# A new order of all steps, and new engines for the elementwise steps, in a kernel of attention and a softplus MLP

## The chip, the cores and the metric

The kernel runs on 1 core of one Trainium2 chip. The metric is device time in microseconds (us), the median of several runs. The profile is one execution, taken by the hardware profiler; its engines are PE (TensorE's matmuls), PEld (its weight loads), DVE (VectorE), ACT (ScalarE), POOL (GpSimd) and SP (SyncE, which issues the DMAs here).

## The reference

Two parts: attention in both directions between 512 tokens and 32 state rows per head, and a two-layer MLP with softplus over all 8 x 544 rows.

```python
def _attn_ref(x, state):               # B, H, S, Ns, D = 8, 8, 512, 32, 64
    scale = 1.0 / np.sqrt(D)
    scores = scale * np.matmul(x, state.transpose(0, 1, 3, 2))
    scores = scores - scores.max(-1, keepdims=True)
    a = np.exp(scores)
    a /= a.sum(-1, keepdims=True) + 1e-09
    xread = np.matmul(a, state)
    scores2 = scale * np.matmul(state, x.transpose(0, 1, 3, 2))
    scores2 = scores2 - scores2.max(-1, keepdims=True)
    a2 = np.exp(scores2)
    a2 /= a2.sum(-1, keepdims=True) + 1e-09
    sread = np.matmul(a2, x)
    return np.concatenate([xread, sread], axis=2).astype(np.float32)

def _moe_ref(x, w_in, w_out):          # x: (8 * 544 rows, 512), d_ff = 2048
    h = x @ w_in
    g = np.maximum(h, 0.0) + np.log1p(np.exp(-np.abs(h)))
    return (g @ w_out).astype(np.float32)

def reference(**kwargs):
...
    x = np.ascontiguousarray(attn_out.transpose(0, 2, 1, 3)).reshape(B * S, H * D)
    return _moe_ref(x=x, **moe_kwargs)
```

The weights w_in and w_out are float64 in memory.

## The kernel before

The work is cut into steps, each of them one or a few instructions on one engine. A step has a letter; each letter stands for a generator function that makes its steps one after another (first g, second g, and so on). The string PLAN names all 1565 steps of the kernel by their letters, in one order. The last loop of the function goes through PLAN and lets the named generator make its next step. Every instruction goes through a helper (line 84) that keeps it in this order on its engine; so each engine, and the DMA queue of SyncE, works off its own steps strictly in the order of PLAN, and waits between engines come only from data and from buffers. No wait holds two engines apart that share no data.

For the letters that stand in ENG, the table gives the engine of each single step: A is ScalarE, D is VectorE, P is GpSimd. All other letters have a fixed engine.

The steps, by what they do:

- Loads (SyncE): S state, T the transposed tokens xT, X the tokens, I w_in, O w_out, in pieces of mostly 512 KB. The weights are loaded as float64 words.
- Weights: the float64 words are made into float32 in three steps. For w_in: a (ScalarE, upper word), b (VectorE, lower word), c (VectorE, joins both into W). For w_out: A, B, C in the same way. Then D makes the rounded high part of w_out (float32r) and E the rest of it, low part, as D by the engine of ENG.
- Scores of one batch: Q (TensorE). Towards tokens: 1 (transpose of 32 x 32 blocks on VectorE), 2 (maximum), 3 (subtract), 4 (exponential), 5 (sum and reciprocal), 6 (multiply), 7 (transpose back), 8 and 9 (high and low part). Towards state: e (maximum), f (exponential), i (reciprocal), t (transpose on TensorE), u (copy), R (matmul with the tokens), r (scale), y (transpose on TensorE), z and Z (high and low part).
- The first product is not computed as (a @ state) @ w_in; v multiplies the state with W (TensorE), h and l split the result into high and low part, and g (gemm1) multiplies that with the attention weights. A product of two split operands takes three matmuls (high x high, high x low, low x high), so one g of 512 columns is six matmuls.
- s is softplus (ScalarE) from PSUM to SBUF, m and n its high and low part, G (gemm2) the second product, two G for one g, each six matmuls; o copies a finished bank of PSUM to SBUF and p stores it.
- For the state rows, w and x split w_in itself, and eight g of 24 matmuls multiply it with the state read.

The order of slots (one slot is a g, an s, an m, an n and two G) is fixed in SLOTS: 16 slots of 128 hidden columns each for batch 0, then batch 1 and so on; before the last batch, the eight slots of the state rows. So batch 0 needs all of w_in and w_out within its 16 slots.

Buffers are rooms with names, taken in the order in which they came free: 27 of 2 KB per partition (tiles s in the profile), 26 of 4 KB (tiles d: raw loads, a's split parts, the split w_out), 5 small ones (v), and 8 banks of PSUM (b). W is the joined w_in, ST the state. With another order, a step can get another room, and so wait for another step.

```python
    run = {k: f() for k, f in steps.items()}
    for k in PLAN:
        now[0] = k
        count[k] = count.get(k, 0) + 1
        next(run[k])
```

Of the kernel before, what the change touches and what calls it, by code (L numbers as in the profile page):

```python
# [19 lines left out]
B, H, S, NS, D = 8, 8, 512, 32, 64  # L20
# [12 lines left out]
UNITS = {0: [(0, 256), (256, 512), (512, 1024), (1024, 1536), (1536, 2048)]}  # L33
UNIT = [(512 * c, 512 * c + 512) for c in range(4)]
PLAN = (
    "STTIQa112eIX2bb345e34ftf6t5a7ccI6uv897XOIIau8ihRiblOa9hlaIcbBgAIgscIvOBCsRhmhlDrlgbAcIrbaCDObcEnbamgIAOGGcacsI"
    "BOnvbsIyOTIChAEhDlIlbEBGmCAnIGOBgmagcCaGaaBbcsgssOAmDIncGBbcgaCaEvnAhDbGmACDazEGBlZCDhlbGsGgnaEmXcOAgAbBgOScGB"
    "AbssmcCnDTsmOEcQBEB1DXT2envO3hfeflnCAEGGGOG1OgihlDtsGECGB4mOuADgAAstT56GCmm2CgnD7sBuv3ERhRn4lir89G5g6EhCAmGn7G"
    "lG8gnmSDrysvzmhnTlEBDGshmElGQGTB1CZ9geg1GDssCEneGm2G34fmgDggsGnnfs5tuEGsnGopGvoohv67ilmmogng2smntmunh3gslmGXG4"
    "igGGhGlnsGhmgG8s5GGXnlTsnRmRrvhGlmgs6grhGGGlgsn7ynmvn9p8smzngZmGGgssGGGhgGlhG9mlsmpGgmGngsnsgmmnGnsgQs1ev2GeGG"  # L40
    "GGhGlmnpf3nGG1holgmpGgssotmgs4nnGfm2GGm34gGsgGoGG5nGToumv5shvnnXmhGGlhpGi6TgGnGsmGng7l6lsGgmng8nisSs9hgtmGGuGn"
    "GGGpmXXG7G8glssmmngGvRnsR9hGlgsGghGlrnsmGrgsvGgXmhpmlggnGGsoThGysoolvQsnhl1e2gGzspZggnef3om4snG1hf5GGggGisGstm"
    "6mmg2ls3nu4GGmtusmmgnGingpGGRRmnsrrm7nvGGGhmGg5nGmh6snp7mpsXGvlhn8yzmG9GGhGGZn8Gl9lngsGmnvhGgnllgGsghGssmggGlX"
    "Q1emTssfvnGTGnheGgomoGnolgs2ogs341GGnGsp5fGgmGg2st6mnmgmnhmGlnsTGsGmnt3pgpuguGn7isGg4smsmmnGgigs56RrRrv7snhmX8"
    "h8vmXGlGGGGG9plnGG9nGGnGgsmhGmgsngsmhnGlmnvyGlGhlzGhGGnggGXZsgGolmGspmvholsoQTn1geegh1sfgslnGn2Gm3ns42GGmGtupg"
    "gomnfgs3tGGGinG4msGgnGGssmimGmn5GnGuGvR5hpRw6lnGG7mgGrGs6GGvm8h9rlnyg7shGgnzGsGxmn8m9GglnhsgmsGGGGnlpgGmsZGooQ"
    "o1vpvhlmmgsp2eowgfnef1gphgssntnglhmGlGpG3nmGmsxmG2hsiG4G3igtGnnw5lunXmx4GwGngsgsggmuGGn6sssGxggG7Gs5RRrm8rwv9y"
    "GxGsGnzmgZGhwsgnwhlmGnGGm6xmGsnnmng7mgxwwsGGxsnwGmxwwG8GgGxmGmxwGnwsnolGxonmGpgxwsgxoxomGGsgGmnnw9sxggGvmvsshh"
    "vGGGlGGnmpnGglsgnmsGgpGhsmgGsnGGmonGmlmhGlGgGnsnhglGgGmGGsomnGgshlGsggmnsGnmnGsgpmgGGnnGgsGGmmGnGssGGgnGGmnGgG"
    "smsnmmGpGnGGnGGoGoooppppp"  # L50
)
ENG = {
    '3': "PPPDDPDPPPDDPDDD",
    '6': "PPPDPPDDPPPDDDDD",
    '8': "APADAPDAAPDADADA",
    '9': "PDDPDPPPPDPPPDPD",
    'D': "PDPPDPPPDPPDAPDA",
    'E': "PPDPPDPPPDPDPDDP",
    'h': "AAAAADAADDAAADDADDDDADAADDDDADDDAAAAAADDDDDADAAAADDADDAAADDDDAAAAD",
    'm': "DPPPDPPPDADPADPDPDPPPPADPAPADPPPDAAPPAPDDADDADAPDDPAADDPPPPAAPADPDPPPDAPDADADADDAPPPAAPPPDPAPPDDPAPAPAPPDPPPPADPADADAAAPDAADAAAAAPDDPDDP",  # L60
    'n': "PDPDPDPDPPPPPDPPDDPPDDDDPDDDDPPDDDPPPDPDPPDPPPPDDPPDPPDDDPDPPPPDPDDDDDDPPPDDPDPDPPPPPDPDDDPDPDDPPPDPPDDDDPPPPPDDPDPPPPDDPPPDDPPPDDDPDPDD",
    'o': "ADAADDAAAADADAADDDAAAAADDAAAADAAAA",
    'r': "DDDDAAAADDDDAAAD",
    'u': "AAAAAADADDADDDDA",
    'w': "DPPDPPDAAPDPPDPD",
    'x': "DDPDDDPDPPPDDPPD",
    'z': "AAAADAAA",
}


# [635 lines left out]
```

## Time and profile before

| | before |
|---|---|
| median of 3 runs | 671.09 us (670.12 to 671.17) |
| the profiled execution | 670.02 us, span 668.2 us |
| TensorE busy | 646.5 us (97%), 3856 matmuls |
| VectorE busy | 293.3 us (44%), 515 instructions |
| ScalarE busy | 249.8 us (37%), 398 instructions, 49 of them table loads |
| GpSimd busy | 204.2 us (31%), 197 instructions |
| read and written | 34.60 MB and 8.91 MB |
| granted TensorE clock | 1.0 |

The span goes from the first to the last instruction of the program. In a group's row stand the line, the engine, the operation, the tiles out<-in, the shape and the count; behind the bar the busy time in us and the mean ns of one; behind the second bar the idle time of the engine just before them, and whose end closed most of it. A row of a table by stretches has the stretch and its length, then for each engine the busy time and the count in the order PE, PEld, DVE, ACT, POOL, then the clock, the DMA engines' share and GB/s. All steps have line 84, that of the helper, so they are told apart by tiles and operations.

### The profile page before, as it was taken

How to read it: one execution, taken by the hardware profiler on the slowest of the kernel's cores; microseconds unless marked ns; L12 is line 12 of the kernel's file. 1: busy time of each engine (PE TensorE's matmuls, PEld its weight loads, DVE VectorE, ACT ScalarE, POOL GpSimd, SP SyncE). 2: the span in 40 equal slices, each digit the busy share in tenths (PEclk: the TensorE clock that was granted, in tenths of full speed). 3: DMA queues.
4: the chain of work that ended last, by engine and by line, in shares of the span. 5: the costliest groups of instructions: out<-in, count | busy, mean ns of one | idle time of the engine just before them, and what ended most of it. 6: DMA issues, size and time to landing. Idle time of an engine off the chain costs nothing.

```text
span 668.2 us, 9510 instructions
## 1 busy us (share of the span) xinstructions
PE 646.5 (97%) x3856; PEld 498.5 (75%) x3856; DVE 293.3 (44%) x515; ACT 249.8 (37%) x398; POOL 204.2 (31%) x197
## 2 busy tenths in 40 slices
PE   2999999999999999999999999999999999999997
PEld 0555767777787877777778777877778798888886
DVE  4999987444325312543264421434265153222110
ACT  2876755622332312732265321811263121313201
POOL 2545553312131420334211411411241456211210
PEclk9999999999999999999999999999999999999999
DMA  8995110500042020301030201100110000001001
GB/s 313 410 404 206 53 32 1 158 1 0 1 141 96 0 79 5 123 26 38 0 112 1 79 0 55 41 0 2 42 53 1 1 1 31 32 1 32 0 1 63
DMA packets 15851, 44.12 MB, mean 66 GB/s; under 512 B 1728, under 2 KB 2752, under 8 KB 15808
## 3 DMA queue, kind: packets, MB, share of 16 engines
q1 hardware_dynamic: 15808, 43.52, 18.3%
q8 instruction: 30, 0.49, 0.3%
q14 instruction: 13, 0.11, 0.0%
HBM read 34.60 MB, written 8.91 MB: 65 GB/s over the span
## 4 chain that ended last, share of the span: by engine, by line
PE 88%; DVE 9%; issue 1%; DMA 1%; ACT 1%; SPq 0%; DVEq 0%
PE b L84 88%; DVE s L84 6%; DVE W L84 1%; DVE v L84 1%; DVE d L84 1%; DMA d<-in_xt_dram 1%; ACT s L84 0%; ACT L84 0%; SPq L84 0%; DVE sreadT L84 0%; DVEq L84 0%
## 5 line engine op out<-in xcount | busy, mean ns | idle before, releaser
L84 PE MATMUL b<-d,s 128*128 128x512 f32 (+1 forms) x2912 | 568.5, 363 | 1.9 <-DVE v L84 1.6
L84 PEld LDWEIGHTS b<-d,s 128*128 128x128 f32 (+1 forms) x2912 | 455.0, 175 | 116.9 <-issue 18.9
L84 ACT ACTIVATE s<-b 128x512 f32<-128x512 f32 x136 | 80.3, 599 | 286.4 <-PE b L84 282.1
L84 POOL TENSOR_TENSOR s<-s,s 128x512 fp32r<-128x512 f32 x72 | 96.9, 1351 | 210.8 <-PE b L84 135.8
L84 POOL TENSOR_SCALAR s<-s 128x512 fp32r<-128x512 f32 x56 | 38.2, 684 | 157.1 <-PE b L84 67.8
L84 ACT ACT_TABLE_LOAD x49 | 62.9, 1283 | 23.4 <-DVE v L84 10.8
L84 DVE TENSOR_TENSOR s<-s,s 128x512 fp32r<-128x512 f32 x64 | 49.2, 772 | 47.9 <-PE b L84 23.3
L84 DVE TENSOR_TENSOR s<-b,s 128x512 fp32r<-128x512 f32 (+1 forms) x66 | 43.7, 665 | 49.7 <-ACT s L84 42.2
L84 DVE CAST s<-s 128x512 fp32r<-128x512 f32 x40 | 20.0, 500 | 67.9 <-ACT s L84 43.4
L84 PE MATMUL b<-W,ST 64*32 64x512 f32 (+1 forms) x528 | 41.9, 592 | 4.0 <-DVE W L84 3.9
L84 DVE CAST s<-b 128x512 fp32r<-128x512 f32 x32 | 21.9, 684 | 50.4 <-PE b L84 50.2
L84 POOL TENSOR_TENSOR d<-s,d 128x512 fp32r<-128x512 f32 x20 | 28.6, 1435 | 16.0 <-DVE d L84 9.8
L84 ACT CAST s<-b 128x512 fp32r<-128x512 f32 (+1 forms) x34 | 19.0, 563 | 34.3 <-PE b L84 34.2
L84 DVE COPY s<-b 128x512 f32<-128x512 f32 x18 | 12.4, 688 | 43.5 <-PE b L84 43.5
L84 POOL TENSOR_TENSOR s<-s,v 128x512 f32<-128x512 f32 x16 | 18.4, 1150 | 38.0 <-DVE v L84 30.9
L84 ACT COPY s<-b 128x512 f32<-128x512 f32 x32 | 18.5, 587 | 26.8 <-PE b L84 22.1
L84 ACT CAST s<-s 128x512 fp32r<-128x512 f32 x40 | 24.4, 620 | 10.5 <-PE b L84 10.2
L84 DVE STREAM_TRANSPOSE s<-b 128x512 f32<-128x512 f32 x16 | 11.2, 708 | 38.7 <-PE b L84 37.0
L84 DVE TENSOR_REDUCE v<-s 128x16 f32<-128x512 f32 x32 | 21.5, 673 | 10.5 <-ACT s L84 10.4
L84 PEld LDWEIGHTS b<-W,ST 64*32 64x32 f32 x528 | 8.5, 106 | 22.7 <-DVE W L84 11.1
L84 PEld LDWEIGHTS b<-sreadT,s 128*128 128x128 f32 x192 | 23.8, 192 | 0.5
L84 PE MATMUL b<-sreadT,s 128*128 128x256 f32 x192 | 24.0, 283 | 0.0
(39 smaller groups left out, 255.0 us busy)
## 6 DMA issues: line engine op xcount, KB each, us to landing
d<-in_xt_dram SPq DMA_DIRECT2D x16, 512.0 KB, 4.7
d<-in_w_in_dram SPq DMA_DIRECT2D x16, 512.0 KB, 10.3
d<-in_xn_dram SPq DMA_DIRECT2D x16, 512.0 KB, 4.5
d<-in_w_out_dram SPq DMA_DIRECT2D x16, 512.0 KB, 10.2
out_dram<-s SPq DMA_DIRECT2D x32, 256.0 KB, 2.2
ST<-in_zp_dram SPq DMA_DIRECT2D x1, 512.0 KB, 9.2
out_dram<-s SPq DMA_DIRECT2D x8, 64.0 KB, 1.7
ST<-in_zp_dram SPq DMA_DIRECT2D x2, 128.0 KB, 4.7
```

What stands on the lines that cost most here:

```text
L84: return lambda *a, **k: self.tc.keep_in_program_order(f(*a, **k))
```

## The change

PLAN is another order of the same 1565 steps: each letter comes as often as before, and the steps of one letter stay in their own order. ENG gives other engines to the steps of 15 letters. Nothing else differs. By the words that came with it, order and engines were made anew, with GpSimd's and VectorE's steps that read only SBUF kept apart in time. Counted over ENG (ScalarE, VectorE, GpSimd): D goes from 2, 5, 9 to 10, 5, 1; 8 from 8, 5, 3 to 6, 1, 9; m from 40, 40, 56 to 38, 54, 44; h from 34, 32, 0 to 39, 27, 0; n from 0, 64, 72 to 0, 63, 73; the others by two or less.

```diff
--- before.py
+++ after.py
@@ -33,38 +33,38 @@
 UNITS = {0: [(0, 256), (256, 512), (512, 1024), (1024, 1536), (1536, 2048)]}
 UNIT = [(512 * c, 512 * c + 512) for c in range(4)]
 PLAN = (
-    "STTIQa112eIX2bb345e34ftf6t5a7ccI6uv897XOIIau8ihRiblOa9hlaIcbBgAIgscIvOBCsRhmhlDrlgbAcIrbaCDObcEnbamgIAOGGcacsI"
-    "BOnvbsIyOTIChAEhDlIlbEBGmCAnIGOBgmagcCaGaaBbcsgssOAmDIncGBbcgaCaEvnAhDbGmACDazEGBlZCDhlbGsGgnaEmXcOAgAbBgOScGB"
-    "AbssmcCnDTsmOEcQBEB1DXT2envO3hfeflnCAEGGGOG1OgihlDtsGECGB4mOuADgAAstT56GCmm2CgnD7sBuv3ERhRn4lir89G5g6EhCAmGn7G"
-    "lG8gnmSDrysvzmhnTlEBDGshmElGQGTB1CZ9geg1GDssCEneGm2G34fmgDggsGnnfs5tuEGsnGopGvoohv67ilmmogng2smntmunh3gslmGXG4"
-    "igGGhGlnsGhmgG8s5GGXnlTsnRmRrvhGlmgs6grhGGGlgsn7ynmvn9p8smzngZmGGgssGGGhgGlhG9mlsmpGgmGngsnsgmmnGnsgQs1ev2GeGG"
-    "GGhGlmnpf3nGG1holgmpGgssotmgs4nnGfm2GGm34gGsgGoGG5nGToumv5shvnnXmhGGlhpGi6TgGnGsmGng7l6lsGgmng8nisSs9hgtmGGuGn"
-    "GGGpmXXG7G8glssmmngGvRnsR9hGlgsGghGlrnsmGrgsvGgXmhpmlggnGGsoThGysoolvQsnhl1e2gGzspZggnef3om4snG1hf5GGggGisGstm"
-    "6mmg2ls3nu4GGmtusmmgnGingpGGRRmnsrrm7nvGGGhmGg5nGmh6snp7mpsXGvlhn8yzmG9GGhGGZn8Gl9lngsGmnvhGgnllgGsghGssmggGlX"
-    "Q1emTssfvnGTGnheGgomoGnolgs2ogs341GGnGsp5fGgmGg2st6mnmgmnhmGlnsTGsGmnt3pgpuguGn7isGg4smsmmnGgigs56RrRrv7snhmX8"
-    "h8vmXGlGGGGG9plnGG9nGGnGgsmhGmgsngsmhnGlmnvyGlGhlzGhGGnggGXZsgGolmGspmvholsoQTn1geegh1sfgslnGn2Gm3ns42GGmGtupg"
-    "gomnfgs3tGGGinG4msGgnGGssmimGmn5GnGuGvR5hpRw6lnGG7mgGrGs6GGvm8h9rlnyg7shGgnzGsGxmn8m9GglnhsgmsGGGGnlpgGmsZGooQ"
-    "o1vpvhlmmgsp2eowgfnef1gphgssntnglhmGlGpG3nmGmsxmG2hsiG4G3igtGnnw5lunXmx4GwGngsgsggmuGGn6sssGxggG7Gs5RRrm8rwv9y"
-    "GxGsGnzmgZGhwsgnwhlmGnGGm6xmGsnnmng7mgxwwsGGxsnwGmxwwG8GgGxmGmxwGnwsnolGxonmGpgxwsgxoxomGGsgGmnnw9sxggGvmvsshh"
-    "vGGGlGGnmpnGglsgnmsGgpGhsmgGsnGGmonGmlmhGlGgGnsnhglGgGmGGsomnGgshlGsggmnsGnmnGsgpmgGGnnGgsGGmmGnGssGGgnGGmnGgG"
-    "smsnmmGpGnGGnGGoGoooppppp"
+    "TSTQI1efI234Sb1iaX2b3ec56III4tfba5XacaOitu67IvbuRh8hIcRIcAv7laO9lb8hhI9bBallcOcgaCObagOTIIrggsbOIcmDscrvEnObsB"
+    "shhABTABaAymIaOllCmDCcGDCbAnDaGngBsgsgzcIEGGbsaZBOEgbOmAcsEcOGCnDGmQvnefeAhBCGAfhDXBCEBDGal1lGaCbBBEmGOc2IgAnm"
+    "gAsCmbgsnictD1gGObnGIsacaBsACEbcEmGG3v4tmS2XuGmhhGSullnADXg5BDAEsO36gCvhERsC7lnTRGrGhDOiE4ClGA8gD5rs6GEmTBmAmn"
+    "7GgyzQZs8vnXBGhGDeE9fenGl9fiGt12ChGmDEmgusnlgGOC1D3sggvGnETmnsA4msBmGCDghGE2msh3GoGgnllpvvnosghlosghmg5pssGGlg"
+    "GnTsngGGn6GGogGsm7h4tG5imsgGlg6X8sgnmnnmGshgsGnmGlsumRrXpmpRnvr7hlmQTee912GG3mn1GfGGG8Xm293tGgsGhnmimunnglfsgG"
+    "4gvm4sGGsnghG5tsGgGsgGGuXgnsGGm65in7oGlRRTnoonhvlsrhmynz89rggpogsGmZgsmGpsGlhmmGGTlnyzvhmGlGng6nGhZsT7GGGsg8lv"
+    "GmsG9ggsghsnnnhsGmGGmggslpsgGGmmGnlsnmnvQGGmGe1GGhfGg2GlnmGn345sniG6mg1GhensgGGosGovT7gpnmlhnslgpghGlgsossgftG"
+    "m8mTug2sG9nGm3m4gptGsnsmgnngGpGGm5GmmGm6GGnGs7msuGmGnoGGnvnhhil89mlvnGhGhglXGRsRGmgGnGmlrsQprveh1lGGGnfGgsgnsm"
+    "gG2nXensgtihGnGGm34snufmgnGo561gltsms7goGnG8GoGimms2ungyovs3RGhzrmGlpZGGGnnGgGhGmsGglRsmr4vhplvGgsG5nGm678TnGg"
+    "GhslhgsnglvshlQ9hGel1G12mmGn9nhGgfg3GGs2mnGmsmGgsgmengsgmplnGGGsmGw3sn4gtnuGnX5m6ggsGopfgonXsppgoTGms4nGGGmGsG"
+    "m7mmvGh5n86nGiGs7tiogul9Rh8RsrrlnvmGmnGG9GhgGsnGyzylnGgGxGmnsGmhlGgGpzgnGsGmmngsGGGgnswGsmnGGXGmmGogoZsvhZQnhl"
+    "pvlhmGongnghse1glolsgeXGfG1p2GgfwsGGx3mitGsnsmuivpgshGtlGgnhlggsRsuRm4nmsGmnrnGGmgpmsGngGmGswgGxr2GymsvzGn3gxG"
+    "GwsnZwgxmmGwgn5xswxnwGGsngwxmmGms6gswxGxnnmGG4wxxnGmGw7gGhpglxhw56l8GmGGsswxoxgnw7s8vhGhG9pmonGxGGgls9nGggmogm"
+    "gspGsslGnGovhnsvlnhmGgggGGmmhssmlGGnGgpnnngGsmmomsmlgGmGnGGGGGnnssoGGgnmGmshnGmnlGgsGgGmGgsgmGnsgGGGsGnnnsGGGG"
+    "pmGGmnGGpnmGGnpGoGpoooppp"
 )
 ENG = {
-    '3': "PPPDDPDPPPDDPDDD",
-    '6': "PPPDPPDDPPPDDDDD",
-    '8': "APADAPDAAPDADADA",
-    '9': "PDDPDPPPPDPPPDPD",
-    'D': "PDPPDPPPDPPDAPDA",
-    'E': "PPDPPDPPPDPDPDDP",
-    'h': "AAAAADAADDAAADDADDDDADAADDDDADDDAAAAAADDDDDADAAAADDADDAAADDDDAAAAD",
-    'm': "DPPPDPPPDADPADPDPDPPPPADPAPADPPPDAAPPAPDDADDADAPDDPAADDPPPPAAPADPDPPPDAPDADADADDAPPPAAPPPDPAPPDDPAPAPAPPDPPPPADPADADAAAPDAADAAAAAPDDPDDP",
-    'n': "PDPDPDPDPPPPPDPPDDPPDDDDPDDDDPPDDDPPPDPDPPDPPPPDDPPDPPDDDPDPPPPDPDDDDDDPPPDDPDPDPPPPPDPDDDPDPDDPPPDPPDDDDPPPPPDDPDPPPPDDPPPDDPPPDDDPDPDD",
-    'o': "ADAADDAAAADADAADDDAAAAADDAAAADAAAA",
-    'r': "DDDDAAAADDDDAAAD",
-    'u': "AAAAAADADDADDDDA",
-    'w': "DPPDPPDAAPDPPDPD",
-    'x': "DDPDDDPDPPPDDPPD",
-    'z': "AAAADAAA",
+    '3': "PPPPPDPPDPDDDPPD",
+    '6': "PPDDDDPPDDPDPPDP",
+    '8': "AAPAPAAPPPPDAPPP",
+    '9': "PDPDPPPDDDPDPDDP",
+    'D': "ADDDAADPAAAAAADA",
+    'E': "DPPDPDPPDPDPDDPD",
+    'h': "AAAAAAAADADDDDADAAADADDDDAAAAADDDDADAADADDDDDDADAAAAAADADAAAAAADAA",
+    'm': "ADDPDPAPAPDDDAPDDDADADPDDDPADDADPPPAAPDADPADDDPDPDPPPAPDPPAPPAPDADDDDPAPAADPPAPADPDPDDAAPDAAADADAAPDDPPAAAAPDADPPDDDDDPPPAPADDPADPADPDDD",
+    'n': "DPDPDPDDPPPPPDPDDPPPPPPPDPDPDPDDDPDPPDDPPDDPDDDPDDDDPPDDDDDDPPDPPPPDPPDPDPPPPPPPPPDDDPPDDPPPDDDDPDPPDDPPDDPPDDPDPPPDPPPDPDDDPDPPDDPPDPPD",
+    'o': "ADADDAAAAADADAADDDADADAAADAADDAAAA",
+    'r': "DADDDDDAAAAAADDD",
+    'u': "AADDADDDADDADDAA",
+    'w': "PDDDPADDAPADPDPP",
+    'x': "PDDDPPPPDDPDDPPP",
+    'z': "DDAAADAA",
 }
```

## The prediction

> **What bounds the kernel now.** I read the page first: the busy shares and the chain of work that ended last.
>
> ```profile
> span 668.2 us, 9510 instructions
> PE 646.5 (97%) x3856; PEld 498.5 (75%) x3856; DVE 293.3 (44%) x515; ACT 249.8 (37%) x398; POOL 204.2 (31%) x197
> PE 88%; DVE 9%; issue 1%; DMA 1%; ACT 1%; SPq 0%; DVEq 0%
> ```
>
> The same chain in order of time ends so:
>
> ```profile
> 104.84 388.56 PE b L84 x2340
> 493.41 171.04 PE b L84 x952
> 664.47 0.59 ACT s L84
> ```
>
> TensorE is busy for 97% of the span, and from 104.84 to the last matmul the chain is TensorE alone; VectorE's 9% lie before. So no change of order can gain anything behind 105 us; it could only lose there. The change adds and removes no matmul. What can move is the opening, and the waits of TensorE (us in total, times, the longest) show too little of it; two rows:
>
> ```profile
> PE b L84 <- DMA d<-in_xt_dram: 5.6, 1, 5.6
> PE b L84 <- DVE W L84: 3.9, 6, 0.8
> ```
>
> The weights W came late six times by 0.8 us at most, by this view. But matmuls that wait between two of one group still count as busy. A steady stretch gives the true pace, and the groups from 130 us on that of the smaller steps:
>
> ```profile
> 594.00:644.00 50.00, 50.00 (x222) 41.43 (x221) 9.28 (x16) 13.50 (x24) 10.60 (x9) 1.00 0.05 11
> ```
>
> ```profile
> L84 PE MATMUL b<-W,ST 64*32 64x512 f32 x384 | 25.0, 597 | 0.0
> L84 PE MATMUL b<-sreadT,s 128*128 128x256 f32 x192 | 24.0, 283 | 0.0
> L84 PE MATMUL b<-d,s 128*32 128x64 f32 x384 | 6.6, 220 | 0.0
> L84 PE MATMUL b<-ident,s 128*128 128x128 f32 x40 | 6.0, 271 | 0.0
> L84 PE MATMUL b<-d,ST 64*32 64x512 f32 x80 | 5.4, 596 | 0.0
> L84 PE MATMUL b<-ident,v 128*64 128x128 f32 x24 | 2.6, 298 | 0.0
> ```
>
> 222 matmuls in 50 us (one cut by the edge) are 0.226 us each, so a step of six (one gemm1, letter g, or half a gemm2 slot, letter G) is 1.36 us. The small rows hold 24 v, 12 R, 10 t, 5 Q and 6 y: 1.04, 0.55, 0.60, 1.08 and 0.43 us each. All work at that pace: 400 x 1.357 + 24.0 + 32 x 1.04 + 16 x 0.55 + 16 x 0.60 + 8 x 1.08 + 8 x 0.43 = 630. The first matmul starts at 5.6 (the DMA row), and 668.2 - 664.5 = 3.7 us of copies and stores follow the last one. The rest, 29 us, is TensorE being late, and that is the sum that the change can draw on.
>
> Who makes TensorE late is seen in the opening's instructions in order of time (start, length, engine). VectorE starts when the first scores are there and then hardly rests:
>
> ```profile
> 9.00 1.31 DVE L84 STREAM_TRANSPOSE s<-b 128x512 f32<-128x512 f32 x2 [9.00 <-PE b L84]
> ...
> 31.96 1.39 POOL L84 TENSOR_TENSOR d<-s,d 128x512 fp32r<-128x512 f32 x1 [1.42 <-DVE d L84]
> 32.13 1.77 DVE L84 SCALAR_TENSOR_TENSOR W<-s,s 128x512 int32<-128x512 int32 x1
> ```
>
> A join of weight words (c) takes 1.77 us, because a GpSimd step began 0.17 before it. Undisturbed, two joins take 1.28, so 0.60 from start to start, and two lower-word steps 0.75:
>
> ```profile
> 34.16 1.28 DVE L84 SCALAR_TENSOR_TENSOR W<-s,s 128x512 int32<-128x512 int32 x2
> ...
> 45.40 0.75 DVE L84 TENSOR_SCALAR s<-d 128x512 int32<-128x512 int32 x2
> ```
>
> Two subtractions that read PSUM beside SBUF run on unhindered beside a GpSimd step:
>
> ```profile
> 37.84 1.27 DVE L84 TENSOR_TENSOR s<-b,s 128x512 fp32r<-128x512 f32 x2
> 37.98 0.62 POOL L84 TENSOR_SCALAR s<-s 128x512 fp32r<-128x512 f32 x1
> ```
>
> And this is where TensorE pays, the last piece of W and the fifth v:
>
> ```profile
> 66.81 0.68 DVE L84 SCALAR_TENSOR_TENSOR W<-s,s 128x512 int32<-128x512 int32 x1
> ...
> 67.54 1.05 PE L84 MATMUL b<-W,ST 64*32 64x512 f32 x4 [0.49 <-DVE W L84]
> ...
> 68.52 7.10 PE L84 MATMUL b<-d,s 128*128 128x512 f32 x30
> ```
>
> The means of all that ran between 9 and 93 us say the same: joins are stretched, reductions (one SBUF input) are not.
>
> ```profile
> L84 DVE SCALAR_TENSOR_TENSOR W<-s,s 128x512 int32<-128x512 int32 x16 | 16.4, 1033 | 0.1
> L84 DVE TENSOR_REDUCE v<-s 128x16 f32<-128x512 f32 x8 | 5.4, 672 | 0.1
> ```
>
> The Trainium skill, page "SBUF — State Buffer", section "Who interferes with whom", gives a reason: VectorE and GpSimd share one pair of SBUF ports, held as a lock for a whole instruction, by VectorE instructions with two SBUF inputs or in a two-port mode, and never by a tensor_reduce. By that rule the two groups above must differ as they do, and the trace agrees (1.77 against 0.68 us; 672 ns unstretched).
>
> **The change part by part.** The kernel's numbers of steps stay; their order in the one list and the engines of the free elementwise steps change. I compare both lists at one place that the trace shows as a real wait: the last piece of w_in (c, the 16th), whose join ends at 66.81 + 0.68 = 67.49 and lets v, the fifth, go on.
>
> VectorE's price up to there, at undisturbed spacings. From the rows: 0.34 for a lower-word step or a cast (0.75 for two, less the 0.41 of the last), 0.60 for a join, subtraction or product, 0.64 for a transpose, 0.67 for a reduction; the small instructions 0.1 to 0.2 each. In the old list 86 steps stand there: 26 b and B (8.8), 25 c and C (15.0), eight l, four of them half wide (3.8), two 1 and two 7 (2.6), two 2 and two e with their small ones (3.0), two 5 (2.1), six two-input steps 9, n, E (3.6), five casts m and D (1.7), and 1.6 of small ones and one h: 42.2. It took 67.49 - 9.00 = 58.5. The difference, 16.3, is nearly all blocking by GpSimd, which has 27 steps up to there: 0.60 us for each. TensorE had 22 steps of six, two Q, two t, four v (two half wide), two R and a y before that v, 37.9 us; its end at 68.52 is 68.5 - 5.6 - 37.9 - 1.0 = 24.0 us late. So 24 of the 29 are gathered here.
>
> In the new list 99 VectorE steps stand before the same join: two more 1, two e, one 2, one i, two B, one C, one E, two n, two D, one z, and one r and one h fewer: 49.2, so 7.0 more. GpSimd has 16 steps there (16.9 us of work) in place of 27 (25.1): six D and six m have become one and three, mostly given to ScalarE. TensorE has three more G, one more g and one more t to do before that v: 4 x 1.36 + 0.60 = 6.0 us of work that is then behind it. So the end moves by (9.0 + 49.2 + X - 67.5) - 6.0 = X - 15.3, where X is what blocking still costs. No row of before shows X. Its ends: 16 steps at the old 0.60 are 9.6; with all apart, 0 (an order can't make VectorE faster than undisturbed, so nothing below). Nothing waits to enforce the distance; GpSimd starts when its input is ready. In the new list GpSimd steps often stand next to steps that don't collide (a product 9 between two l; E next to Z and h), but also some between two joins. I take the middle, 4.8: **-10.5 us**. With X near 0 another place holds the gain: the first g needs about 12.7 us of VectorE work (11.9 before), and TensorE has 4.4 us to do ahead of it (Q, two t, two half v, two R), so it is 9.0 + 12.7 - 5.6 - 4.4 = 11.7 late there. Against 24.0, no more than about 12 can be gained by this.
>
> ScalarE pays for this. Its prices:
>
> ```profile
> L84 ACT ACT_TABLE_LOAD x49 | 62.9, 1283 | 23.4 <-DVE v L84 10.8 <-issue 7.1 <-DVE s L84 4.7
> L84 ACT ACTIVATE s<-b 128x512 f32<-128x512 f32 x136 | 80.3, 599 | 286.4 <-PE b L84 282.1
> L84 ACT ACTIVATE s<-d 128x512 f32<-128x512 f32 x32 | 19.5, 670 | 7.0 <-DMA d<-in_w_in_dram 7.0
> L84 ACT CAST s<-s 128x512 fp32r<-128x512 f32 x40 | 24.4, 620 | 10.5 <-PE b L84 10.2
> 8.99:78.70 69.71, 59.25 (x351) 38.67 (x352) 68.00 (x116) 48.52 (x76) 35.25 (x33) 1.00 0.79 302
> 9.00:20.00 11.00, 3.28 (x16) 1.63 (x16) 10.79 (x19) 5.95 (x12) 5.74 (x5) 1.00 1.04 409
> ```
>
> ```profile
> 75.81 4.38 PE L84 MATMUL b<-d,s 128*128 128x512 f32 x18
> ```
>
> The thirteenth g needs the last split of group 0's products (h, l). It is the last six of the 18 matmuls from 75.81, so it starts at 75.81 + 12 x 0.226 = 78.5. Up to there ScalarE was busy 48.5 of 69.7 us. In the new list it has to do, before that l: 27 a and A (27 x 0.67 = 18.1), 12 s (7.2), 10 table loads (12.8; a load is due wherever softplus and the exponential or word steps change places), 9 h, four of them half wide (4.4), 8 casts 8, m, D (4.9), 4 f and 3 of step 4 (exponentials as long as the word steps, and a short read behind each f; 5.4), 2 u and an r (1.4): 54.2. The stretch 9 to 20 had 11.00 - 5.95 = 5.05 idle on it, caused by the first loads and the first scores, which stay. With that idle alone: 9.0 + 54.2 + 5.05 + 0.6 for the l behind it = 68.9, and TensorE has one G less and one t more before this g, 0.76 less: 68.9 - 78.5 + 0.8 = **-8.8 us**. The later of the two chains sets the end, so -8.8.
>
> Over the whole list, table loads rise from 49 to 55 (counted from the order of ScalarE's steps): 6 x 1.283 = 7.7 us, all but a few behind 105 us, hidden under TensorE; ScalarE is busy 37% there. If that cover were gone it would cost the 7.7. The moved engines behind 105 us cost nothing for the same reason. One thing is tighter: two v stand only 3.7 and 4.6 us of TensorE work before the g that needs them (least 14 before, past the opening). The chain h, l, l is about 0.60 + 2 x 0.60 = 1.8, so it holds with one step queued ahead; with three it costs about 1 us. I take 0.
>
> DMA: w_in's last piece is the 38th transfer in place of the 31st.
>
> ```profile
> 34.85 0.33 SPq L84 DMA_DIRECT2D d<-in_w_in_dram x1
> d<-in_w_in_dram SPq DMA_DIRECT2D x16, 512.0 KB, 10.3
> ```
>
> It landed about 34.85 + 10.3 = 45.2. Transfers of 0.5 MB at 409 GB/s (the last column of the 9 to 20 stretch, above) are 1.28 us, so seven places are 9 us: 54.2. VectorE reaches its b, just ahead of the join, at about 9.0 + 48.0 + X = 57.0 + X: hidden by 2.8 us plus X; its room is free then (it waits for the eleventh b, 30 us of VectorE work in). The tail (four copies, stores) is the same in both lists.
>
> The sum stands against the profiled run, 670.02 with a span of 668.2; the median of the runs shown is 671.09, 1.07 above it. The shift taken off the median: 671.1 - 8.8 = 662.3.
>
> **The rivals.**
> - Blocking per GpSimd step stays as it was, 0.60: X = 9.6, so -5.7: 665.4. For it: no wait keeps the engines apart. Against: eight of the eleven GpSimd steps taken out are casts D and m from the stretch in which VectorE joins weights.
> - The chains are better than forecast: X near 0 and ScalarE's opening idle halved (2.5): -12: 659, and to 657 if the 5 us of lateness gathered after 68 us shrink too.
> - Slower: ScalarE becomes the bound. If it idles as much before the thirteenth g as it did (69.7 - 48.5 = 21.2), that g starts at 9.0 + 54.2 + 21.2 + 0.6 = 85.0: +7.3, 678. It decides from 5.05 + 8.8 = 13.9 us of idle on. Against: most of that idle was waiting for TensorE and VectorE, which were late from blocking.
> - The order doesn't keep them apart at all: every GpSimd step stops VectorE for its whole length. X = 16.9: +1.6, 672.7. Against: in the old list 25.1 us of GpSimd work cost 16.3, not 25.1. The lock that the Trainium skill's page "SBUF — State Buffer" (same section) describes would give this where VectorE has only colliding steps at hand; the 37.84 row shows that it often has others.
> - Loads late by more than they are hidden: no change or worse; 670.
>
> **How the numbers follow.** Forecast (660 to 665) 0.55; blocking unchanged 0.17; better 0.13; ScalarE bound 0.08; whole-length blocking 0.04; loads 0.03. The range 656.5 to 668 holds the first three, 0.85, and ends short of the others. Faster by over 0.2% (1.3 us, about what this kernel's timing can tell): 0.85; slower: 0.08 + 0.04 = 0.12, of which 0.01 I give to within 0.2% with the 0.03: same 0.04, slower 0.11.
>
> **What would show it.** In the changed profile: the join before the fifth v ends near 63.0 (9.0 + 49.2 + 4.8) in place of 67.49; mean of the W joins between 9 and 93 us near 0.8 in place of 1.033; ScalarE idle under 10 us up to the thirteenth g, 55 table loads, and TensorE without a wait behind 105 us. Joins still at 1.0 would make the first step wrong; ScalarE idle above 14, the second; a TensorE wait behind 130 us would make the cover wrong.

## The result, and the profile after

| | before | after |
|---|---|---|
| median of 4 runs | 670.89 us (670.12 to 671.17) | 663.85 us (663.05 to 664.38) |
| the profiled execution | 670.02 us, span 668.2 | 663.05 us, span 661.3 |
| ratio of the times | | 0.9896, 95% interval 0.9879 to 0.9913 |

The changed kernel is 7.0 us faster. The forecast was 662.3 in a range of 656.5 to 668, so the time was met within 1.6 us. The way to it was not: the opening gained 5.2 us where the forecast had 8.8, 1.8 us that it had not foreseen came later, and the chain that it named as the last one was the wrong one. The page of the kernel after, busy shares, shares of the chain that ended last, and the group of table loads:

```profile
span 661.3 us, 9487 instructions
PE 642.2 (97%) x3856; PEld 496.9 (75%) x3856; DVE 295.0 (45%) x526; ACT 260.8 (39%) x408; POOL 193.4 (29%) x182
PE 91%; DMA 4%; DVE 3%; ACT 1%; issue 1%; SPq 0%; DVEq 0%; ACTq 0%
L84 ACT ACT_TABLE_LOAD x55 | 70.6, 1283 | 32.9 <-DVE s L84 15.6
```

TensorE holds 91% of the chain in place of 88%; VectorE's 9% have become 3%, and 4% of DMA are new. The same chain in order of time (start, length, what) shows where:

```profile
35.81 10.33 DMA d<-in_w_out_dram
46.16 9.70 DMA ST<-in_zp_dram
55.85 0.40 DVE s L84
...
67.58 0.70 DVE W L84
...
68.33 589.15 PE b L84 x3512
...
657.50 0.58 ACT s L84
```

From 68.33 on the chain is TensorE alone, where before it was so from 104.84. Just ahead of that stands a join of W on VectorE, as before. The DMA pieces of the chain held nothing up: the step of VectorE at 55.85 is the eleventh lower word of w_out, whose piece was issued at 35.81 and landed at 46.14; the state load named behind it landed at 56.08, when that step had already begun; and VectorE's waits in the opening name no DMA. The opening in order of time, VectorE, GpSimd and what bears on them:

```profile
9.74 0.72 DVE L84 STREAM_TRANSPOSE s<-b 128x512 f32<-128x512 f32 x1 [9.74 <-PE b L84]
...
34.18 1.67 POOL L84 TENSOR_TENSOR d<-s,d 128x512 fp32r<-128x512 f32 x1 [1.41 <-DMA d<-in_w_in_dram]
...
34.61 1.79 DVE L84 SCALAR_TENSOR_TENSOR W<-s,s 128x512 int32<-128x512 int32 x1
...
42.21 0.33 SPq L84 DMA_DIRECT2D d<-in_w_in_dram  x1
...
58.49 3.15 POOL L84 TENSOR_TENSOR d<-s,d 128x512 fp32r<-128x512 f32 x2
58.98 1.51 DVE L84 TENSOR_SCALAR s<-d 128x512 int32<-128x512 int32 x1
60.42 1.77 DVE L84 TENSOR_TENSOR s<-s,s 128x512 fp32r<-128x512 f32 x1
61.60 1.50 POOL L84 TENSOR_TENSOR s<-s,v 128x512 f32<-128x512 f32 x1
...
62.37 1.28 DVE L84 SCALAR_TENSOR_TENSOR W<-s,s 128x512 int32<-128x512 int32 x1
...
65.35 0.92 POOL L84 TENSOR_SCALAR s<-s 128x512 fp32r<-128x512 f32 x1 [2.24 <-DVE s L84]
...
65.71 0.83 DVE L84 TENSOR_SCALAR s<-d 128x512 int32<-128x512 int32 x1
...
67.06 0.41 DVE L84 TENSOR_SCALAR s<-d 128x512 int32<-128x512 int32 x1
67.58 0.69 DVE L84 SCALAR_TENSOR_TENSOR W<-s,s 128x512 int32<-128x512 int32 x1
...
68.33 1.05 PE L84 MATMUL b<-W,ST 64*32 64x512 f32 x4 [1.43 <-DVE W L84]
```

The last join of w_in ends at 68.27, 0.8 us later than before (67.49), but TensorE has done 6.0 us more work ahead of it. So TensorE is 5.2 us less late there. And blocking has not gone: at 34.61 a join again takes 1.79 us, because a subtraction of GpSimd (the second E) began 0.43 us before it.

To see all of VectorE's opening at once I split it, for each kernel, from the start and length of its instructions. Work is the sum of the undisturbed start-to-start spacings of all VectorE instructions up to the last join of w_in; idle is the time in which VectorE had nothing that it could start; blocked is what remains. The border between blocked and idle is an estimate, good to some 0.7 us. Late is where TensorE stands behind 5.6 us plus its work so far, at the pace used in the prediction. Of GpSimd's steps two counts are given: those that stand ahead of the last join in PLAN, and in brackets those that had started by the time it ended. All times in us:

```
                    start  work  blocked  idle  join ends  in list (ran)  late, 21st g  late, end
before               9.00  41.3   15.7    1.4    67.5        27 (28)       27.5        28.3
after                9.74  48.2    8.7    1.5    68.3        16 (19)       19.8        21.3
after, run again     9.01  48.2    8.7    1.6    67.5        16 (19)       19.1        20.6
old order, new eng.  8.71  42.6    9.8    5.7    66.9        16 (17)       27.9        29.2
new order, old eng.  9.73  46.6   12.5    2.8    71.7        27 (29)       24.7        29.3
before, fills        9.33  42.1    5.2    1.7    58.4        27 (28)       15.7        16.6
after, fills        10.94  48.4    3.4    2.3    65.2        16 (19)       16.7        18.3
after, no tables     9.66  48.2    9.2    0.7    67.8        16 (19)       18.5        19.8
before, E n on V.    8.82  46.7    5.8    2.1    63.6        18 (18)       24.5        25.4
after, E n on V.    10.36  52.4    2.8    4.0    69.6         9 (11)       22.7        24.3
after, state first   8.76  48.2    8.7    1.6    67.3        16 (19)       18.9        20.3
after, casts on S.  10.35  45.6   10.3    3.8    70.2        16 (19)       21.8        23.3
after, swap          8.57  50.0    4.8    5.9    69.3        16 (18)       24.1        25.5
after, late old eng.10.19  48.2    8.7    1.5    68.7        16 (19)       20.2        24.9
```

The last two columns are read so: after is 7.7 us less late than before at the 21st g, and 7.0 at the end, which is the measured gain. By stages, the gain is 5.2 at the fifth v and 2.5 more up to the 21st g; 0.7 is given back behind it.

GpSimd's steps up to the join are not the ones that the list puts there. The stretch from 9 us to the end of the join, before and then after (the last pair ahead of the clock is GpSimd):

```profile
9.00:67.48 58.48, 48.09 (x300) 30.11 (x300) 57.12 (x95) 40.82 (x64) 29.89 (x28) 1.00 0.90 349
9.00:68.27 59.27, 49.87 (x332) 33.38 (x328) 56.99 (x111) 46.39 (x76) 23.39 (x19) 0.94 0.91 354
```

In the new kernel 19 steps ran there, not 16: the eighth E (60.17, the second of the two from 58.49), the third step 3 (61.60) and the tenth m (65.35) stand behind the join in PLAN and ran ahead of it. By how much they stretched the steps at 60.42, 62.37 and 65.71, they cost VectorE about 2.1 us. By the steps that ran, blocking fell from 15.7 / 28 = 0.56 us each to 8.7 / 19 = 0.46, and it fell in one stretch only. Groups of VectorE between 9 and 28.5 us, before and then after (busy us, mean ns of one):

```profile
L84 DVE SCALAR_TENSOR_TENSOR W<-s,s 128x512 int32<-128x512 int32 x5 | 6.0, 1206 | 0.0
```

```profile
L84 DVE SCALAR_TENSOR_TENSOR W<-s,s 128x512 int32<-128x512 int32 x8 | 5.2, 685 | 0.0
```

Five joins at 1206 ns against eight at 685, the undisturbed length. Up to the eighth join, five GpSimd steps blocked VectorE for 0.2 us in the new kernel; eleven steps blocked it for 5.4 in the old one. From there on a step costs the same in both: 8.5 us for 14 steps in the new kernel and 10.3 for 17 in the old one, 0.61 each.

### The profile page after: what moved, and what is told of

The parts are those of the page before. It is cut to its first block, busy times and chain, and to the rows that moved or that the text cites. A ratio compares the mean times of both kernels' runs of the same rounds, so it can differ in the third digit from the quotient of the medians.

```text
span 661.3 us, 9487 instructions
## 1 busy us (share of the span) xinstructions
PE 642.2 (97%) x3856; PEld 496.9 (75%) x3856; DVE 295.0 (45%) x526; ACT 260.8 (39%) x408; POOL 193.4 (29%) x182
## 4 chain that ended last, share of the span: by engine, by line
PE 91%; DMA 4%; DVE 3%; ACT 1%; issue 1%; SPq 0%; DVEq 0%; ACTq 0%
PE b L84 91%; DMA d<-in_w_out_dram 2%; DMA ST<-in_zp_dram 1%; DVE s L84 1%; DMA d<-in_xt_dram 1%; DVE v L84 1%; ACT s L84 1%; DVE W L84 1%; DVE d L84 0%; ACT L84 0%; ACT d L84 0%; SPq L84 0%; DVEq L84 0%; ACTq L84 0%
## 5 line engine op out<-in xcount | busy, mean ns | idle before, releaser
L84 DVE TENSOR_TENSOR s<-s,s 128x512 fp32r<-128x512 f32 x63 | 52.0, 831 | 76.3 <-PE b L84 52.5
L84 POOL TENSOR_SCALAR s<-s 128x512 fp32r<-128x512 f32 x44 | 30.4, 692 | 140.6 <-PE b L84 73.6
L84 DVE CAST s<-s 128x512 fp32r<-128x512 f32 x54 | 35.1, 651 | 47.0 <-PE b L84 36.6
L84 DVE COPY s<-b 128x512 f32<-128x512 f32 x22 | 15.0, 684 | 60.5 <-PE b L84 56.2
L84 PE MATMUL b<-W,ST 64*32 64x512 f32 (+1 forms) x528 | 39.3, 593 | 1.7 <-DVE W L84 1.4
L84 ACT CAST s<-b 128x512 fp32r<-128x512 f32 (+1 forms) x39 | 21.4, 567 | 38.0 <-PE b L84 37.9
L84 ACT COPY s<-b 128x512 f32<-128x512 f32 x28 | 16.2, 589 | 41.6 <-PE b L84 41.2
L84 DVE CAST s<-b 128x512 fp32r<-128x512 f32 x27 | 18.4, 683 | 29.9 <-PE b L84 29.9
L84 POOL TENSOR_TENSOR d<-s,d 128x512 fp32r<-128x512 f32 x16 | 22.8, 1428 | 13.8 <-ACT d L84 8.3
L84 DVE STREAM_TRANSPOSE s<-s 128x512 f32<-128x512 f32 x16 | 11.3, 705 | 26.1 <-PE b L84 26.0
```

The source lines that it names most:

```text
L84: return lambda *a, **k: self.tc.keep_in_program_order(f(*a, **k))
```

## The experiments

The open questions: is blocking by GpSimd what makes the opening late; do the order and the engines each bring a part of the gain; does ScalarE's chain set the end, as the forecast had it; and does the part behind 105 us really cost nothing.

**Engines alone, order alone.** The first kernel has the old PLAN with the new ENG, the second the new PLAN with the old ENG.

```diff
 # old order, new engines: before, with
-ENG = {...}        # of before
+ENG = {...}        # of after
 # new order, old engines: before, with
-PLAN = (...)       # of before
+PLAN = (...)       # of after
```

> The old PLAN with the new ENG. Theory (the gain comes from fewer and cheaper GpSimd steps in the opening): up to the last join of w_in, 16 GpSimd steps stand instead of 27, and four E and three n, which cost VectorE 0.9 us each in the traces, instead of five and four; so VectorE's blocked time there falls from 15.7 to about 9 us, and the time to 664 to 666 us. Rival (the order alone makes the gain, by putting more TensorE work ahead of the late v): blocked time stays near 15 and the time at 669 to 671 us.

Measured: 671.77 us, ratio 1.0031 (1.0017 to 1.0045). Slower than before, though blocking fell to 9.8 us as in the full change. VectorE's waits between 9 and 68 us (total, times, longest) say where this went:

```profile
DVE s L84 <- ACT s L84: 5.3, 6, 2.1
```

VectorE idled 5.7 us in place of 1.4: the old order put its next step behind a ScalarE step that now came later. The last join ends at 66.9, 0.6 before the old kernel's, and the 0.6 are gone by the 21st g.

> The new PLAN with the old ENG, the other corner. Theory (engines): 27 GpSimd steps before the last join again, blocked time about 13 to 15 us, 669 to 671 us. Rival (order): 663 to 665 us as with both changes.

Measured: 672.68 us, ratio 1.0031 (1.002 to 1.0042). Also slower. Here 27 GpSimd steps block VectorE for 12.5 us, and TensorE waits for GpSimd itself (TensorE's waits, whole span):

```profile
PE b L84 <- POOL d L84: 3.9, 2, 3.1
```

The median is 8.8 us above after; of the 8.0 between the two profiled executions, 4.9 are there by the 21st g and 3.1 are gathered behind it. So neither half brings a part of the gain; the 7 us belong to the pair.

**Blocking taken out.** GpSimd's first two-input steps (3, 6, 9, E, n; 27 of them in the old list, 26 in the new) are replaced by a fill, which reads no SBUF.

```diff
     def elementwise(dst, a, b, op, e):
+        if e == "P" and pool_steps[0] < 27:   # 26 in the new list
+            pool_steps[0] += 1
+            nc.gpsimd.memset(f32(dst), 0.001)
+            return
```

> The kernel before, with GpSimd's first 27 two-input steps (3, 6, 9, E, n; all up to about 110 us) replaced by a fill of the same destination with 0.001: GpSimd then reads no SBUF there, which leaves those subtractions and products out. Theory (the reads of GpSimd stop VectorE): blocked time before the last join falls from 15.7 to 3 to 5 us (the casts' share), TensorE is late by about 15 instead of 22 at the fifth v, 658 to 662 us. Rival (any GpSimd use of SBUF blocks, or VectorE's blocked time doesn't set the end): over 668 us.

Measured: 658.53 us, ratio 0.9825 (0.9806 to 0.9844), 12 us faster than before.

> The kernel after, with its first 26 two-input GpSimd steps replaced by fills in the same way. Theory: blocked time before the last join falls from 8.7 to 1 to 2 us; the time falls by 4 to 6 us to 658 to 660 us, so both lists end within 3 us of one another once GpSimd doesn't read. Rival (ScalarE or the order is what holds the new list): under 2 us less, 662 to 664.

Measured: 659.70 us, ratio 0.9835 (0.982 to 0.985), 3 to 4 us faster than after; blocking is 3.4 us, more than the 1 to 2 that were expected. The joins' groups between 9 and 93 us, first of the old list with fills, then of the new one:

```profile
L84 DVE SCALAR_TENSOR_TENSOR W<-s,s 128x512 int32<-128x512 int32 x16 | 11.6, 732 | 0.1
```

```profile
L84 DVE SCALAR_TENSOR_TENSOR W<-s,s 128x512 int32<-128x512 int32 x16 | 10.9, 700 | 0.4 <-ACT s L84 0.3
```

The joins go from 1033 to 732 ns in the old list. Blocking falls by 10.5 us there and by 5.3 in the new list, lateness at the end by 11.7 and 3.0. A fill is also shorter than the step it replaces (562 to 590 ns), so GpSimd is done earlier; but VectorE had idled only 1.4 us in all, so earlier results can't explain 10.5. Once GpSimd's two-input steps no longer read SBUF, the old and the new list end within 1.2 us of one another: the gain of the change is, to that measure, less blocking.

**ScalarE's work made smaller.** Exponential in place of softplus, which needs no change of table beside the other exponentials.

```diff
-            nc.scalar.activation(tt[k].t, hb[k].t, AF.Softplus)
+            nc.scalar.activation(tt[k].t, hb[k].t, AF.Exp)
```

> The kernel after with the exponential in place of softplus (so softplus is left out): all of ScalarE's functions are then in one set, and the 55 table loads, 70.6 us of ScalarE, go. Theory (VectorE, not ScalarE, holds the opening): ScalarE gets 10 loads, 12.8 us, less before the thirteenth g and only idles longer; the time changes by less than 1.5 us, 662.5 to 665. Rival (the recorded step: ScalarE's chain sets the end): 3 to 6 us less, 658 to 661.

Measured: 662.13 us, ratio 0.9879 (0.9864 to 0.9893); 1.7 us less than after, and 0.6 less than after run again. The stretch up to the thirteenth g (busy us of PE, PEld, DVE, ACT, POOL), first after, then this kernel:

```profile
9.00:72.70 63.70, 54.25 (x353) 36.41 (x350) 61.42 (x118) 50.81 (x84) 25.89 (x22) 0.95 0.87 338
```

```profile
9.00:72.10 63.10, 54.66 (x353) 37.26 (x350) 61.76 (x118) 38.30 (x74) 27.03 (x22) 1.00 0.88 342
```

ScalarE has 12.5 us less to do, and the g comes 0.6 us earlier; its rows show not one table load behind the start of the program. ScalarE does not set the end.

**What E and n cost from either engine.** In both kernels the E and n among the first eight of each letter go to VectorE.

```diff
 # before
-    'E': "PPDPPDPPPDPDPDDP",     'n': "PDPDPDPDPPPP...",
+    'E': "DDDDDDDDPDPDPDDP",     'n': "DDDDDDDDPPPP...",
 # after
-    'E': "DPPDPDPPDPDPDDPD",     'n': "DPDPDPDDPPPP...",
+    'E': "DDDDDDDDDPDPDDPD",     'n': "DDDDDDDDPPPP...",
```

> The kernel before with the six E and four n that GpSimd does up to the fifth v given to VectorE. Theory (each of them stops VectorE for 0.9 to 1.0 us by its reads, and VectorE does it itself in 0.60): 6 us more work, 9.6 us less blocked, so 3 to 4 us less late at the fifth v: 666 to 668 us. Rival (VectorE's own work sets it, blocking overlaps with slack): 6 us more work shows as 2 to 6 us longer: 672 to 676.

Measured: 667.39 us, ratio 0.9956 (0.9944 to 0.9967). In the old list each of six E on GpSimd blocked VectorE for 0.91 us and each of four n for 1.02, while VectorE does one itself in 0.60. Moved, they add 5.4 us of work and take away 9.9 of blocking; 3 us are gained.

> The kernel after with its five E and three n of GpSimd up to the fifth v given to VectorE. Theory: 4.8 us more work against 6.4 us less blocked: 1 to 2 us less, 661.5 to 663. Rival (the order and the engines must fit one another, as the two mixed kernels showed): VectorE's steps come late for others, 664 to 668.

Measured: 668.75 us over 12 runs (665.89 to 670.41), ratio 0.9968 (0.9956 to 0.9981): 5 to 6 us slower than after. The two shortest, 665.9, had a granted clock of 1.00, the other ten 0.988 to 0.997; the profiled execution is one of the two, so it can show only some 3 us of the loss. Blocking fell there too, from 8.7 to 2.8, but now TensorE waits for E, which stands in VectorE's queue:

```profile
PE b L84 <- DVE d L84: 7.0, 3, 3.1
```

The three are a G each, behind the second, the fifth and the seventh E.

Less blocking is not by itself less time: in the new list GpSimd's E came in time for its G, and VectorE's did not.

**Is there more to gain by hand?** Three kernels start from after, with the state load first in the queue (S ahead of the first T). One has only that. One gives three m, four D and a z to ScalarE as well. One swaps: E and n to VectorE, m and D to GpSimd.

```diff
 # state first
-    "TSTQI1...
+    "STTQI1...
 # casts on ScalarE, with state first
-    'D': "ADDDAADPAAAAAADA",  'm': "ADDPDPAP...",  'z': "DDAAADAA",
+    'D': "AAAAAAAPAAAAAADA",  'm': "AAAPAPAP...",  'z': "ADAAADAA",
 # swap, with state first
-    'D': "ADDDAADPAAAAAADA",  'E': "DPPDPDPPDPDPDDPD",  'm': "ADDPDP...",  'n': "DPDPDPDD...",
+    'D': "APPPAAPPAAAAAADA",  'E': "DDDDDDDDDPDPDDPD",  'm': "APPPPP...",  'n': "DDDDDDDD...",
```

> The kernel after with the first two letters of PLAN exchanged (S T T in place of T S T, the order of the loads before). Theory: in the profile after, the second half of xT landed at 7.8 in place of 7.0 us and VectorE started at 9.74 in place of 9.00; with the state first both come back: 0.5 to 1 us less. Rival (the start of VectorE varies by more than that from one execution to the next, from 8.71 to 10.94 in the profiles so far, and the order of these three loads isn't the cause): no difference to the kernel after, within 0.3 us.

Measured: 662.02 us, ratio 0.9874 (0.9862 to 0.9887), 1.8 us below the first measurement of after. To see what that is worth, after itself was run again:

> The kernel after once more, unchanged, beside the two below: all theories expect 662.5 to 664.5 us.

Measured: 662.77 us, ratio 0.9886 (0.9872 to 0.9899). VectorE's first transpose in the profile, state first and then after run again:

```profile
8.76 0.72 DVE L84 STREAM_TRANSPOSE s<-b 128x512 f32<-128x512 f32 x1 [8.76 <-PE b L84]
```

```profile
9.01 0.72 DVE L84 STREAM_TRANSPOSE s<-b 128x512 f32<-128x512 f32 x1 [9.01 <-PE b L84]
```

The same kernel, after, started VectorE at 9.74 in one profile and at 9.01 in the other: in the first, TensorE began its scores 0.14 us later and waited 0.23 for a load in the middle of them. The intervals of the two kernels overlap: whether the order of the loads gains anything is not settled.

> The kernel after with the state loaded first, and the eight casts (three m, four D, one z) that VectorE does up to the fifth v given to ScalarE. Theory (VectorE's total work sets the opening, ScalarE has room: it stood idle for 12.9 of 63.6 us): 2.7 us less VectorE work, so 1 to 2.5 us less than with the state load alone: 659.5 to 661.5. Rival (each list of engines fits its order alone; ScalarE is in order and the casts come late): 662 to 667.

Measured: 664.21 us, ratio 0.9902 (0.9888 to 0.9917); 2.2 us more than state first. VectorE has 2.6 us less work; in this profile it starts 1.6 us later than with the state first alone (10.35 against 8.76), as its first loads came late, and it waits for ScalarE (VectorE's waits between 9 and 80 us):

```profile
DVE s L84 <- ACT s L84: 3.2, 3, 2.0
```

> The kernel after with the state loaded first, and up to the fifth v the five E and three n of GpSimd exchanged for the three m and four D of VectorE. Theory by blocked time alone (E and n cost VectorE 0.9 us each from GpSimd and 0.60 as its own; casts 0.25 and 0.34): late by about 2.5 us less, 659 to 661. Rival (what counts is when a step ends for TensorE: E stands behind other VectorE work, as when E and n went to VectorE alone): TensorE waits for the tiles d of VectorE, 664 to 670.

Measured: 667.00 us, ratio 0.9948 (0.993 to 0.9966). Blocking is 4.8, but VectorE idles 5.9 and TensorE waits for E again:

```profile
PE b L84 <- DVE d L84: 7.2, 4, 3.0
```

None of these edits, made with the order left as it is but for the first loads, brought a gain over after that the runs can tell.

**Engines behind 105 us.** After up to the 21st g, and from there the engines of before (239 entries of ENG).

```diff
-ENG = {...}        # of after
+ENG = {...}        # of after for each step up to the 21st g in PLAN, of before behind it
```

> The new PLAN, with the new ENG up to the 21st g (about 108 us) and the old ENG from there on: 239 steps get another engine. Theory (the recorded step that engines chosen behind 105 us cost nothing, being hidden under TensorE): as the kernel after, 662 to 664.5. Rival (order and engines fit one another late too; in the new order with all old engines TensorE gathered 10 us of lateness between the 17th g and the 113th in place of 7): TensorE waits behind 130 us, 665 to 668.

Measured: 666.90 us, ratio 0.9947 (0.9934 to 0.9961): 3 to 4 us slower than after, with the same opening (blocked 8.7, idle 1.5). TensorE's waits between 105 and 655 us, of which after has none:

```profile
PE b L84 <- ACT s L84: 1.2, 2, 0.7
```

The table above counts 4.7 us of lateness from the 21st g on, against 1.5 in after. Only 1.2 of it is shown as waits. TensorE's late starts place 3.2 us of it: 0.70 ahead of the 37th g, 0.82 ahead of the 69th, 1.16 behind the seventh Q, 0.5 behind the 28th v.

## Why the prediction was right, and where it was not

**TensorE is the bound, and nothing is gained behind 105 us: held.** After, nothing waits there and the gain is all gathered by the 21st g. The sum that could be drawn on, 29 us of lateness, also held: 28.3 by the finer count, of which 7.0 went.

**VectorE's chain to the last join: right mechanism, X mis-sized.** The step took X = 4.8, the middle of 0 and 9.6, for a join at 63.0. It ended at 68.27. The terms: blocking 8.7 in place of 4.8 (+3.9), 1.5 us of idle that the step did not have, a start at 9.74 in place of 9.0 (+0.7), and 1.0 less work than counted (48.2 against 49.2); 5.1 of the 5.3. Run again, with a start at 9.01, the join ends at 67.54. Of the 3.9 us by which X was too low, about 2.1 are the three GpSimd steps that the sum did not count, because it took the list's 16. So the shift at the fifth v was -5.2, close to the rival "blocking per GpSimd step stays as it was" (-5.7), and not -10.5. Its reason for a lower price, that eight of the eleven steps taken out were casts D and m, points the other way: casts were the cheap ones. In the old kernel a D blocked VectorE for 0.22 us and an m for 0.30, an E for 0.91 and an n for 1.02. What stayed on GpSimd was the dear kind (E 0.88, n 0.66 after). The signal named for it, W joins near 0.8 in place of 1.033, came true, from two parts: joins of 685 ns up to 28 us, and behind it two blocked ones (1.79 us at 34.61, 1.28 at 62.37). Groups of VectorE after, between 9 and 93 us:

```profile
L84 DVE SCALAR_TENSOR_TENSOR W<-s,s 128x512 int32<-128x512 int32 x16 | 12.4, 790 | 0.1
L84 DVE TENSOR_REDUCE v<-s 128x16 f32<-128x512 f32 x8 | 5.4, 674 | 0.0
```

A mean near the forecast did not mean that the forecast's cause was right: it counts only the joins of w_in, and not the joins of w_out, the lower-word steps, the cast and the subtraction that were blocked behind 28 us.

**ScalarE as the later chain, -8.8: fell.** The step gave ScalarE 5.05 us of idle up to the thirteenth g; it had 63.70 - 50.81 = 12.9, above the 10 that the prediction named as a limit and under the 13.9 from which its rival would decide. The g started at 72.6, not at 68.9. Against before (78.7), with TensorE's 0.76 less work, that is -5.3, the same as VectorE's shift: ScalarE's chain followed VectorE's. With 12.5 us of ScalarE's work gone the g moved by 0.6. So "the later of the two chains sets the end" named the wrong chain.

**Why the time held all the same.** At the fifth v 5.2 were gained in place of 8.8. Between there and the 21st g the old kernel lost 3.5 us more and the new one 1.0, which the sum had left at zero (the rival "better" had it as a possibility); behind it 0.7 was lost. In the old kernel most of it stands ahead of the 15th and the 17th g, where TensorE waited for VectorE again:

```profile
88.65 7.09 PE L84 MATMUL b<-d,s 128*128 128x512 f32 x30 [1.63 <-DVE v L84]
...
103.20 1.17 PE L84 MATMUL b<-d,s 128*128 128x512 f32 x4 [0.23 <-DVE s L84]
```

With fills in the old list it is gone: from the 13th to the 21st g lateness grows by 0.4 us there, and by 3.4 in the kernel before. So this part, too, goes with GpSimd's two-input steps. The whole is -5.2 - 2.5 + 0.7 = -7.0. The 3.6 us too much and the 1.8 too little offset one another in part, so the closeness of the value is partly luck; the range held both.

**Table loads, two close leads, the tail: held.** 55 loads as counted; no wait of TensorE behind 105 us, so the leads of 3.7 and 4.6 us were enough.

**DMA: held, with more to spare than thought.** It had w_in's last piece land at 54.2, hidden by 2.8 us plus X, which is 11.5 with the X measured. The piece was issued at 42.21 and landed at 52.56; VectorE's step on it began at 67.06, 14.5 us later.

**"The moved engines behind 105 us cost nothing": held for this list, false as a reason.** TensorE being the bound and the others under 45% busy was given as the cover. The last experiment has the same cover and lost 3 to 4 us. So idle time alone does not protect that part; that each step's engine has to fit the order would explain the loss, but the runs do not show at which steps it arises, beyond the late starts listed above.

**Whole-length blocking and late loads: did not happen.** Blocking was 8.7 us, where that rival had 16.9; GpSimd was busy for 23.4 us in that stretch.

What stays open: why the two engines are apart up to 28 us and not behind. The trace points to one cause. Whenever a GpSimd step starts up to 28 us, it stands at most 7 places of PLAN ahead of the step that VectorE is at; from 31.46 us to the last join it stands 11 to 29 places ahead, and each of the ten stretched VectorE steps there has beside it a GpSimd step that PLAN puts 9 to 26 places later. So behind 28 us the order of the list was not the order in time. A kernel that holds GpSimd to its place was not run, so it is not shown that this would take the blocking away.

## What to carry to other kernels

Where VectorE and GpSimd both work from SBUF, price a GpSimd step by what it blocks as well as by its own length: here a two-input step of 128x512 (E, n) cost VectorE 0.9 to 1.0 us of blocking on average in the old list, more than the 0.60 of doing it itself, while a cast cost 0.2 to 0.3. Count the steps of the other engine by the time at which they run: nothing holds them to their place in a common list, and here three more ran than the list has. But an order and its engines are one thing: each half of this change alone made the kernel slower than before, and the old engines in a stretch where TensorE seemed to cover everything made it 3 to 4 us slower than after. When a forecast takes the middle between two ends, measure that term by itself (a fill in place of a read does it) before the total is trusted.

## What the runs showed of the hardware that was not expected

**A step that only writes left the joins alone, but not the lower-word steps.** GpSimd's fills in the old list, groups between 9 and 68 us:

```profile
L84 POOL MEMSET s<- 128x512 f32 x10 | 5.8, 590 | 19.4 <-DVE v L84 18.6 <-DVE s L84 0.8
L84 POOL MEMSET d<- 128x512 f32 x8 | 4.4, 562 | 0.0
```

Beside them VectorE's joins take 732 ns. The Trainium skill, page "SBUF — State Buffer", section "Who interferes with whom", says that a VectorE instruction with two SBUF inputs contends with a GpSimd instruction that reads SBUF and not with one that only writes it; these runs agree (732 against 1033 ns). Fills did stretch lower-word steps, which have one SBUF input: four that had only fills beside them took 0.70 to 0.83 us in place of 0.42. One of the four:

```profile
27.15 0.53 POOL L84 MEMSET d<- 128x512 f32 x1
27.25 0.70 DVE L84 TENSOR_SCALAR s<-d 128x512 int32<-128x512 int32 x1
```

**The blocked engine can be GpSimd, for long.** The kernel with the old order and the new engines, in order of time:

```profile
44.02 0.42 DVE L84 TENSOR_SCALAR s<-d 128x512 int32<-128x512 int32 x1
...
44.25 5.76 POOL L84 TENSOR_TENSOR s<-s,s 128x512 fp32r<-128x512 f32 x1 [2.45 <-DVE s L84]
44.35 0.69 DVE L84 SCALAR_TENSOR_TENSOR W<-s,s 128x512 int32<-128x512 int32 x1
...
47.50 0.69 DVE L84 SCALAR_TENSOR_TENSOR W<-s,s 128x512 int32<-128x512 int32 x1
48.10 0.76 DVE L84 TENSOR_SCALAR s<-d 128x512 int32<-128x512 int32 x2
...
48.90 1.66 DVE L84 SCALAR_TENSOR_TENSOR W<-s,s 128x512 int32<-128x512 int32 x1
```

A GpSimd subtraction took 5.76 us while VectorE ran ten instructions back to back from 44.35 at undisturbed length. By the times it got on only when VectorE had rested for 0.04 us, between 48.86 and 48.90; the next join then took 1.66. The same section of that page says that issue order decides who blocks, and that the other is blocked for a whole instruction; here the other was blocked for ten. Yet in the kernel after, at 34.18, a GpSimd subtraction came in between two VectorE instructions with no rest between them and the join at 34.61 paid. What decides between the two is open.

**The clock in the opening.** After's profile has a granted TensorE clock of 0.69 between 9 and 20 us (the third number from the end):

```profile
9.00:20.00 11.00, 4.84 (x52) 1.94 (x52) 9.99 (x26) 6.21 (x14) 4.66 (x4) 0.69 1.04 407
```

Before had 1.00 there, and so had after run again, and the kernel without table loads up to the thirteenth g. The chain of that stretch runs over VectorE, and no cost of it can be seen in the table of the opening: the blocked, idle and work terms are those of after run again.
